# A chunked RWKV-7 and GELU-MLP kernel: the MLP cut into eight pieces between the small products of the next chunk, and the first two inverses on two engines

**Chip, cores, metric.** One core of one Trainium2 chip. The metric is the device time of one execution in microseconds (us). A time quoted is the median of a kernel's runs. Every profile is of one execution; all that the text rests on are of the fast state unless it says otherwise.

## The reference

Four sequences of 768 steps, eight heads of 40. A recurrence per head, then an MLP with an exact GELU over the 320 features:

```python
for t in range(S):
    y[:, :, t] = np.einsum('bhd,bhde->bhe', rt, state)
    Sa = np.einsum('bhde,bhe->bhd', state, at)
    state = state * wt[:, :, None, :] - np.einsum('bhd,bhe->bhde', Sa, bt)
    state = state + np.einsum('bhd,bhe->bhde', vt, kt)
x = y.transpose(0, 2, 1, 3).reshape(B * S, H * D)
h = x @ w_in                                   # 320 -> 2048
out = (0.5 * h * (1.0 + erf(h / sqrt(2)))) @ w_out   # 2048 -> 320
```

## The kernel before

The steps are taken in 12 chunks of 64. In a chunk the recurrence is matrix products plus the inverse of a triangular matrix made of `N`. The names that the argument needs:

- `N`: 64 small products on TensorE, masked on VectorE, stored to DRAM by 8 DMAs, read back as `Nb`.
- the inverse: 62 dependent small operations on GpSimd give `W`; `W` is stored to DRAM (`inv`), read back as `Tt` and `T2`; VectorE transposes a part of it into `L`; TensorE makes `J` from `L` and `J2` from `J`, which completes `Tt`.
- the small stages that use it: `X`, `RV`, `sap`, `saT`, `A`, `M`, `y2`, `QY`, then `xt`, the input of the MLP, made on VectorE and rearranged by DMAs from SP and ScalarE.
- the MLP: `ph` (4 x 40 products of `xt` with `w_in`), gelu on ScalarE, `po` (two halves of 32 products with `w_out`), copied to `os` and stored.
- for the chunk after: loads of w, a, k, b, v, r (32 DMA issues, all on SP), `sums` (the products `cum`, copied to `cs`), transposes `wT`, `aT`, `nT`, `kT`, `vT`, `rT`, `tn`.

The order of TensorE and of SP (the engine that issues DMAs) is that of the program text. VectorE, ScalarE and GpSimd get their order from the scheduler at build time.

```python
def invert(c):
    Nb = work.tile([P, BL, BL], FP32, tag="Nb", name="Nb")        # one buffer per tag
    W = work.tile([P, BL // 2, BL], FP32, tag="W", name="W")
    ...                                                            # Nb <- DRAM on SP
    for j in range(BL - 1):
        tmp = work.tile([P, BL * BL // 7], FP32, tag="tmp", name="tmp")
        ...
        nc.gpsimd.tensor_tensor(t, W[...], Nb[...], ALU.mult)
        nc.gpsimd.tensor_tensor(W[:, :rows, j + 1:], W[:, :rows, j + 1:], t, ALU.add)

def down(c, g):                                                    # up(c): the four ph groups
    po = duo("po")[:, 0, :DM]
    for f in range(NF):
        nc.tensor.matmul(po, gts[c][:, f, g * P:(g + 1) * P], w_out_sb[:, f], ...)
    os = work.tile([P, DM], FP32, tag="os", name="os")
    nc.vector.tensor_copy(os, po)
    ...                                                            # two stores on SP
```

The loop (`n` is the next chunk, `n + 1` the one after; the conditions at the ends are cut):

```python
for c in range(NCH):
    make_N(n); invert(n)
    load_wa(n + 1)
    make_X(c); make_RV(n); make_sa(c); make_A(n)
    make_M(c); make_y2(c); make_QY(c, 0); make_QY(c, 1)
    outputs(c)                                  # xt and the state
    make_av(n)
    down(c - 1, 1)
    load_kb(n + 1); load_v(n + 1); load_r(n + 1)
    up(c)
    sums(n + 1)
    fetch_inverse(n)                            # store W, load Tt and T2, all on SP
    down(c, 0)
    corner(n)                                   # L and J
    turns_a(n + 1); turns_b(n + 1); turn_state()
    joined(n)                                   # J2
```

## Time and profile before

| before | | read from |
|---|---|---|
| time | 936.18 us (935.42 to 937.65, 3 runs) | the runs |
| TensorE busy | 759.0 us, 81% | page, part 1 |
| one chunk, steady | 69.44 us | VectorE's time order: the masks of `N` of chunks 3 and 11 start at 260.90 and 816.40, over 8 |
| mask of `N` of chunk 2 | 193.11 | the same |
| from the mask of chunk 11 to the end | 118.8 | 935.2 - 816.40 |
| `ph` idle for `xt` | 19.0 us in all | page, part 5 |

The "period" below is always that third line, from each kernel's own trace. It is a measure that does not mix the start and the end with the steady chunks. The chain and the queue of one chunk are in the prediction. One thing more is needed later, the end of the inverse on TensorE, from its time order (start, duration, instruction, and in brackets the idle time before it and what ended it):

```profile
457.95 0.74 PE L98 MATMUL J<-L,N 32*32 32x32 f32 x64 [2.53 <-DVE L L428]
458.62 1.75 PE L282 MATMUL wT_ps<-ident,cs_pad 128*128 128x128 f32 x8
460.64 1.88 PE L282 MATMUL aT_ps<-ident,a_pad 128*128 128x128 f32 x8 [0.27 <-ACT part L274]
```

TensorE stands for 2.5 us until L is there, and the two groups of transposes after it take 1.75 and 1.88 us, where the five groups after them take 1.04.

### The profile page before, as it was taken

The page shows a single profiled execution, that of the slowest core. Times are in us where ns is not written, and L with a number is a line of the kernel's source. Part 1 is how long each engine was busy: PE and PEld are TensorE (multiplying, and loading weights), DVE is VectorE, ACT ScalarE, POOL GpSimd, SP SyncE. Part 2 cuts the span into 40 slices and gives each one's busy share as a digit, 9 for nine tenths or more (in the row PEclk, how much of TensorE's full clock was granted, in tenths as well). Part 3 has the DMA queues.
Part 4 walks back from the last instruction along what each step waited for, and adds up shares of the span by engine and source line. Part 5 has one row for each costly group of instructions (what it writes and reads, how often), then busy time and mean ns, then how long its engine had stood idle before and what let it go on. Part 6 is the DMA issues. An engine that isn't in the chain of part 4 may idle for free.

```text
span 935.2 us, 29736 instructions
## 1 busy us (share of the span) xinstructions
PE 759.0 (81%) x13256; PEld 640.0 (68%) x13256; DVE 301.5 (32%) x414; ACT 199.2 (21%) x225; POOL 341.8 (37%) x842
## 2 busy tenths in 40 slices
PE   4343638279879989889889879889899899889898
PEld 3232636278668778688678778778788688778785
DVE  2666788150150240240240250250340330330200
ACT  3020011022222221221221221221322221211110
POOL 4382180118228127127137128127136136136000
PEclk9555769599999979979979889889979979889999
DMA  8677434324233233233233233234233233121100
GB/s 139 116 123 104 93 101 115 58 58 71 48 66 66 46 66 67 45 66 67 45 67 69 43 66 69 42 66 72 41 75 68 38 77 67 32 50 21 24 22 14
DMA packets 255246, 60.40 MB, mean 65 GB/s; under 512 B 241232, under 2 KB 250960, under 8 KB 255120
## 3 DMA queue, kind: packets, MB, share of 16 engines
q1 hardware_dynamic: 251040, 56.22, 32.8%
q10 hardware_dynamic: 4080, 2.30, 1.2%
q8 instruction: 104, 1.70, 0.8%
q14 instruction: 22, 0.18, 0.1%
HBM read 44.30 MB, written 10.22 MB: 58 GB/s over the span
## 4 chain that ended last, share of the span: by engine, by line
PE 52%; SPq 14%; DMA 11%; issue 8%; POOL 6%; DVE 6%; ACT 2%; DVEq 0%; POOLq 0%; ACTq 0%
PE ph L573 15%; PE po L578 13%; SPq L144 5%; PE QY L98 4%; POOL W L397 3%; POOL tmp L395 3%; DMA inv<-W 3%; SPq L414 3%; DMA Tt<-inv 2%; DMA gt<-in_moe_w_in_dram 2%; SPq L133 2%; PE aT_ps L282 2%; SPq L357 2%; PE y_ps L98 2%; PE M_ps L98 2%
## 5 line engine op out<-in xcount | busy, mean ns | idle before, releaser
L395 POOL TENSOR_TENSOR tmp<-W,Nb 128x126 f32<-128x126 f32 (+22 forms) x372 | 143.1, 385 | 282.8 <-DMA Nb<-N 254.6
L573 PE MATMUL ph<-xt,w_in_sb 64*128 64x256 f32 x1920 | 212.1, 379 | 19.0 <-DMA xt<-xt 19.0
L573 PEld LDWEIGHTS ph<-xt,w_in_sb 64*128 64x128 f32 x1920 | 187.0, 188 | 44.3 <-DVE low L231 19.1
L578 PE MATMUL po<-w_out_sb,gt 128*128 128x320 f32 x768 | 212.8, 435 | 2.1 <-DVE w_out_sb L233 2.1
L578 PEld LDWEIGHTS po<-w_out_sb,gt 128*128 128x128 f32 x768 | 144.9, 190 | 62.7 <-DVE w_out_sb L233 2.6
L397 POOL TENSOR_TENSOR W<-W,tmp 128x126 f32<-128x126 f32 (+22 forms) x372 | 147.8, 397 | 29.2
L428 DVE STREAM_TRANSPOSE L<-Tt 128x512 f32<-128x512 f32 x12 | 8.5, 712 | 295.6 <-DMA Tt<-inv 295.6
L570 ACT ACTIVATE gt<-ph 128x1024 f32<-128x1024 f32 x48 | 49.2, 1024 | 222.4 <-PE ph L573 222.4
L302 POOL TENSOR_TENSOR ks<-k_raw,part 128x640 f32<-128x640 f32 x12 | 24.3, 2024 | 86.6 <-ACT part L274 86.6
L98 PE MATMUL J<-L,N 32*32 32x32 f32 x768 | 10.3, 208 | 48.2 <-DVE L L428 48.2
L98 PEld LDWEIGHTS J<-L,N 32*32 32x32 f32 x768 | 9.2, 120 | 54.3 <-issue 53.1
L580 DVE COPY os<-po 128x320 f32<-128x320 f32 x24 | 11.7, 487 | 103.2 <-PE po L578 103.2
L274 ACT ACT_TABLE_LOAD x12 | 15.4, 1283 | 121.6 <-DVE cs_pad L272 121.6
L98 PE MATMUL QY<-VR,ks 64*64 64x104 f32 x768 | 35.4, 340 | 5.4 <-issue 5.4
L98 PEld LDWEIGHTS QY<-VR,ks 64*64 64x64 f32 x768 | 31.8, 198 | 6.8 <-issue 6.8
L387 POOL MEMSET W<- 128x512 f32 x12 | 6.7, 561 | 72.7 <-DMA inv<-W 72.7
L526 DVE TENSOR_TENSOR y<-QY,y 128x512 f32<-128x512 f32 x22 | 15.1, 686 | 54.1 <-PE QY L98 42.0
L98 PE MATMUL cum<-w_raw,cum_m 128*128 128x320 f32 x48 | 18.4, 512 | 12.2 <-DMA k_raw<-in_k_dram 9.3
L318 POOL COPY VR<-v_pad 128x320 f32<-128x320 f32 x24 | 11.1, 472 | 44.4 <-DMA v_pad<-in_v_dram 44.4
L98 PE MATMUL M_ps<-rT,saT 40*64 40x64 f32 x768 | 22.3, 261 | 5.9 <-issue 4.3
L487 ACT COPY saT<-saT_ps 128x512 f32<-128x512 f32 x12 | 7.0, 586 | 92.9 <-issue 80.9
L98 PE MATMUL saT_ps<-Tt,part 64*64 64x64 f32 x704 | 20.2, 271 | 6.9 <-issue 6.9
(105 smaller groups left out, 1004.2 us busy)
## 6 DMA issues: line engine op xcount, KB each, us to landing
Nb<-N SPq DMA_DIRECT2D x24, 256.0 KB
wo_raw<-in_moe_w_out_dram SPq DMA_DIRECT2D x16, 320.0 KB
w_raw<-in_w_dram SPq DMA_DIRECT2D x48, 80.0 KB
k_raw<-in_k_dram SPq DMA_DIRECT2D x48, 80.0 KB
b_raw<-in_b_dram SPq DMA_DIRECT2D x48, 80.0 KB
v_pad<-in_v_dram SPq DMA_DIRECT2D x96, 40.0 KB
r_pad<-in_r_dram SPq DMA_DIRECT2D x96, 40.0 KB
out_dram<-os SPq DMA_DIRECT2D x48, 80.0 KB
```

The costliest lines, as they stand in the source:

```text
L98: nc.tensor.matmul(o, lhsT, rhs, start=first, stop=True, skip_group_check=True)
L133: eng.dma_start(out=t[half(e), g], in_=rows_of(src, c, g, e))
L144: eng.dma_start(out=t[half(e), g, y::2, :D], in_=rows[:, NP * y:NP * (y + 1)])
L282: nc.tensor.transpose(pt[:, g, n], src(g, n), ident)
L302: nc.gpsimd.tensor_tensor(ks[:, :, :, :D], raws.pop((c, "k")), rwv, ALU.mult)
L357: nc.sync.dma_start(out=blk[x, e, z].rearrange("n s t -> s n t"), in_=N[at:at + BL, x, :, :, z * BL:(z + 1) * BL].rearrange("p g n t -> p ...
L395: nc.gpsimd.tensor_tensor(t, W[:, :rows, j:j + 1].to_broadcast([P, rows, rest]), Nb[:, j:j + 1, j + 1:].to_broadcast([P, rows, rest]), ALU ...
L397: nc.gpsimd.tensor_tensor(W[:, :rows, j + 1:], W[:, :rows, j + 1:], t, ALU.add)
L414: nc.sync.dma_start(out=flat_T[at + z * BL:at + (z + 1) * BL, x, :, z * BL:(z + 1) * BL], in_=inv[x, e, z].rearrange("n s t -> s n t"))
L570: nc.scalar.activation(gt[:, 4 * q:4 * q + 4].rearrange("p (s x) t -> p x s t", x=2), ph, ACT.Gelu)
L573: nc.tensor.matmul(o, lhsT, rhs, start=kt == 0, stop=kt == NK - 1)
L578: nc.tensor.matmul(po, gts[c][:, f, g * P:(g + 1) * P], w_out_sb[:, f], start=f == 0, stop=f == NF - 1)
```

## The change

The intent: put dense MLP work between the small products, so that TensorE neither waits for their evacuation nor loses its clock. The MLP of a chunk becomes a generator of 8 pieces, and `fill()` puts one into the order of TensorE. The pieces go "a chunk behind": the last four stand between the small stages of the next chunk. All loads move ahead of `xt`. At the start, the inverse of chunk 0 goes to VectorE so that it can run beside that of chunk 1 on GpSimd.

```diff
-    def invert(c):
+    def invert(c, eng):             # GpSimd's operations become eng's
...
+    def mlp(c):
+        for q in range(NF // 4):
+            ...                     # 40 ph products, gelu
+            yield
+        for g in range(G):
+            ...                     # 16 po products, yield, 16 more, os, stores
+            yield
...
-        if more:
+        if more and c:
             make_N(n)
-            invert(n)
-        if more2:
-            load_wa(n + 1, nc.sync)
+            invert(n, nc.gpsimd)
         make_X(c)
+        fill()
+        if more2:
+            load_w(n + 1); load_a(n + 1); load_kb(n + 1); load_v(n + 1); load_r(n + 1)
         if more:
             make_RV(n)
         make_sa(c)
+        fill()
+        make_saT(c)
         if more:
             make_A(n)
+        fill()
         make_M(c)
         make_y2(c)
+        fill()
         make_QY(c, 0)
         make_QY(c, 1)
         outputs(c)
+        if c == 0:
+            first_convert(4); second_weights(0, 8)
+        pieces.append(mlp(c))
+        fill()
         if more:
             make_av(n)
-        if c:
-            down(c - 1, 1)
-        ...                         # loads of k, b, v, r
-        up(c)
         if more2:
             sums(n + 1)
+        fill()
         if more:
             fetch_inverse(n)
-        down(c, 0)
+        if more2:
+            turns_a(n + 1)
+        fill()
         if more:
             corner(n)
         if more2:
-            turns_a(n + 1)
             turns_b(n + 1)
         if more:
             turn_state()
+        if c == 0:
+            second_weights(8, NF)
+        fill()
+        if more:
             joined(n)
```

The start is reordered as well: `invert(0, nc.vector)`, the loads and `N` of chunk 1 right behind it, `invert(1, nc.gpsimd)`, and the conversion of the weights mostly after `joined(0)`. `N` of chunk 1 gets another buffer; `Nb`, `W` and `tmp` do not. Cut here.

More of the change, by code (lines that the diff above doesn't have):

```diff
@@ L147, in fetch_padded, with load_w, load_a @@
         raws[c, n] = t
-    def load_wa(c, other):
+    def load_w(c):
         fetch(c, "w", w, nc.sync)
-        fetch_padded(c, "a", a, other, False)
+    def load_a(c, eng=nc.sync):
+        fetch_padded(c, "a", a, eng, False)
     def load_kb(c):
@@ L155, in load_kb, with load_v @@
         fetch(c, "b", b, nc.sync)
-    def load_v(c):
-        fetch_padded(c, "v", v, nc.sync, True)
+    def load_v(c, eng=nc.sync):
+        fetch_padded(c, "v", v, eng, True)
     def load_r(c):
@@ L163 @@
     ctx.enter_context(tc.manual_schedule(engines={mybir.EngineType.PE, mybir.EngineType.SP}))
-    load_wa(0, nc.scalar)
+    load_w(0)
+    load_a(0, nc.scalar)
     load_kb(0)
@@ L185 @@
     ks_ring, nb_ring = (ring(n, 2, [P, G, H, HP], pads, nc.gpsimd) for n in ("ks", "nb"))
-    N_ring = ring("N", 1, [P, 2, G, NP, C], None, None)
     VR_ring = ring("VR", 2, [P, 2, G, NP, VC], None, None)
@@ L349, in make_N @@
         t = turned_in[c]
-        N = t["N"] = N_ring()
+        N = t["N"] = work.tile([P, 2, G, NP, C], FP32, tag="turned" if c == 1 else "N", name="N")
         masked(flat(N), products("N_ps", t["nT"], t["aT"], True))
@@ L386, in invert @@
         W = work.tile([P, BL // 2, BL], FP32, tag="W", name="W")
-        nc.gpsimd.memset(W, 0.0)
+        eng.memset(W, 0.0)
         for par in range(2):
             nc.sync.dma_start(out=Nb[par * n:(par + 1) * n], in_=blk)
-            nc.gpsimd.memset(W[par * n:(par + 1) * n].rearrange("p s t -> p (s t)")[:, par::BL + 2][:, :BL // 2], 1.0)
+            eng.memset(W[par * n:(par + 1) * n].rearrange("p s t -> p (s t)")[:, par::BL + 2][:, :BL // 2], 1.0)
         for j in range(BL - 1):
@@ L394, in invert @@
             t = tmp[:, :rows * rest].rearrange("p (s t) -> p s t", s=rows)
-            nc.gpsimd.tensor_tensor(t, W[:, :rows, j:j + 1].to_broadcast([P, rows, rest]),
+            eng.tensor_tensor(t, W[:, :rows, j:j + 1].to_broadcast([P, rows, rest]),
                                     Nb[:, j:j + 1, j + 1:].to_broadcast([P, rows, rest]), ALU.mult)
-            nc.gpsimd.tensor_tensor(W[:, :rows, j + 1:], W[:, :rows, j + 1:], t, ALU.add)
+            eng.tensor_tensor(W[:, :rows, j + 1:], W[:, :rows, j + 1:], t, ALU.add)
         inverses[c] = W
@@ L480, in make_sa, with make_saT @@
                               sap.rearrange("p x y g a d -> p x (y g a) d"))
+    def make_saT(c):
+        t = turned_in[c]
+        xs, Tt = t["xs"], t["Tt"]
         pt = duo("saT_ps").rearrange("p r (k x t) -> p r k x t", k=G * NA, x=2)
@@ L558 @@
     gts = {}
-    def up(c):
+    def mlp(c):
         xt = xts.pop(c)
-        gt = gts[c] = gt_tile()
+        gt = gt_tile()
         for q in range(NF // 4):
@@ L568, in up, with fill @@
                     for x in range(2):
-                        mm_up(ph[:, x, s], w_in_sb[half(x), kt, p * P:(p + 1) * P], xt[half(x), kt], kt)
+                        nc.tensor.matmul(ph[:, x, s], w_in_sb[half(x), kt, p * P:(p + 1) * P], xt[half(x), kt],
+                                         start=kt == 0, stop=kt == NK - 1)
             nc.scalar.activation(gt[:, 4 * q:4 * q + 4].rearrange("p (s x) t -> p x s t", x=2), ph, ACT.Gelu)
-    def mm_up(o, lhsT, rhs, kt):
-        nc.tensor.matmul(o, lhsT, rhs, start=kt == 0, stop=kt == NK - 1)
-    def down(c, g):
-        po = duo("po")[:, 0, :DM]
-        for f in range(NF):
-            nc.tensor.matmul(po, gts[c][:, f, g * P:(g + 1) * P], w_out_sb[:, f], start=f == 0, stop=f == NF - 1)
-        os = work.tile([P, DM], FP32, tag="os", name="os")
-        nc.vector.tensor_copy(os, po)
-        for e in range(2):
-            row = (G * g + e) * S + c * C
-            nc.sync.dma_start(out=out[row:row + C], in_=os[half(e)])
-    first_load(0)
-    first_load(1)
-    load_v(0)
-    sums(0)
-    turns_a(0)
-    make_N(0)
-    invert(0)
+            yield
+        for g in range(G):
+            po = duo("po")[:, 0, :DM]
+            for f in range(NF):
+                nc.tensor.matmul(po, gt[:, f, g * P:(g + 1) * P], w_out_sb[:, f], start=f == 0, stop=f == NF - 1)
+                if f == NF // 2 - 1:
+                    yield
+            os = work.tile([P, DM], FP32, tag="os", name="os")
+            nc.vector.tensor_copy(os, po)
+            for e in range(2):
+                row = (G * g + e) * S + c * C
+                nc.sync.dma_start(out=out[row:row + C], in_=os[half(e)])
+            yield
+    pieces = []
+    def fill(n=1):
+        while n and pieces:
+            if next(pieces[0], "end") == "end":
+                pieces.pop(0)
+            else:
+                n -= 1
+    first_load(0)
+    load_v(0, nc.scalar)
+    sums(0)
+    load_w(1)
+    turns_a(0)
+    load_kb(1)
+    make_N(0)
+    load_a(1)
+    invert(0, nc.vector)
+    first_load(1)
     load_r(0)
+    sums(1)
+    turns_a(1)
+    make_N(1)
+    invert(1, nc.gpsimd)
     turns_b(0)
@@ L596 @@
     make_av(0)
-    first_convert(0)
-    first_load(2)
-    first_convert(1)
-    load_wa(1, nc.sync)
-    load_kb(1)
-    first_load(3)
-    sums(1)
-    turns_a(1)
+    fetch_inverse(0)
     load_v(1)
-    first_convert(2)
-    first_load(4)
     load_r(1)
     turns_b(1)
-    first_convert(3)
-    first_convert(4)
-    fetch_inverse(0)
-    corner(0)
-    joined(0)
-    second_weights(0, 4)
+    corner(0)
+    first_convert(0)
+    first_convert(1)
+    joined(0)
+    first_load(2)
+    first_convert(2)
+    first_load(3)
+    first_convert(3)
+    first_load(4)
     for c in range(NCH):
@@ L618 @@
         more, more2 = n < NCH, n + 1 < NCH
-        if more:
+        if more and c:
             make_N(n)
-            invert(n)
+            invert(n, nc.gpsimd)
+        make_X(c)
+        fill()
         if more2:
-            load_wa(n + 1, nc.sync)
-        make_X(c)
+            load_w(n + 1)
+            load_a(n + 1)
+            load_kb(n + 1)
+            load_v(n + 1)
+            load_r(n + 1)
         if more:
@@ L627 @@
         make_sa(c)
+        fill()
+        make_saT(c)
         if more:
             make_A(n)
+        fill()
         make_M(c)
         make_y2(c)
+        fill()
         make_QY(c, 0)
         make_QY(c, 1)
+        outputs(c)
         if c == 0:
-            second_weights(4, 8)
-        outputs(c)
+            first_convert(4)
+            second_weights(0, 8)
+        pieces.append(mlp(c))
+        fill()
         if more:
             make_av(n)
-        if c == 0:
-            second_weights(8, NF)
-        if c:
-            down(c - 1, 1)
-        if more2:
-            load_kb(n + 1)
-            load_v(n + 1)
-            load_r(n + 1)
-        up(c)
         if more2:
             sums(n + 1)
+        fill()
         if more:
             fetch_inverse(n)
-        down(c, 0)
+        if more2:
+            turns_a(n + 1)
+        fill()
         if more:
@@ L659 @@
             turn_state()
+        if c == 0:
+            second_weights(8, NF)
+        fill()
+        if more:
             joined(n)
-    down(NCH - 1, 1)
+    fill(1000)
 _INS = ['r', 'k', 'v', 'w', 'a', 'b', 'moe_w_in', 'moe_w_out']
```

## The prediction

> **What bounds the kernel now.** I read the page, then the chain of waits, then the time order of TensorE and of the DMA-issuing queue (SP) through one steady chunk.
>
> ```profile
> PE 759.0 (81%) x13256; PEld 640.0 (68%) x13256; DVE 301.5 (32%) x414; ACT 199.2 (21%) x225; POOL 341.8 (37%) x842
> PEclk9555769599999979979979889889979979889999
> ```
>
> The reader is to see that TensorE is busy but not full, and that no other engine is near its limit. The clock row dips once per chunk: TensorE is slowed there as well as idle.
>
> The chain of waits, in order of time, around one steady chunk:
>
> ```profile
> 398.21 1.09 PE N_ps L98 x64
> ...
> 446.81 8.63 PE po L578 x32
> 455.43 0.10 SPq L414
> 455.53 0.04 issue
> 455.57 1.69 DMA Tt<-inv
> ...
> 466.89 0.68 PE J L98 x50
> 467.57 1.09 PE N_ps L98 x64
> ```
>
> N comes at 398.21 and again at 467.57: one chunk takes 69.4 us. Over the nine chunks from N at 191.53 to N at 814.81 the mean is 69.25. Dense MLP work is some 35.2 of it (ph 17.5, po twice 8.8). The rest is small products, at 0.9 to 1.1 us a stage where the clock is full (N above) and about 1.7 where it is half. If all were dense and fast, a chunk would cost about 56: 35.2, eleven stages of 1.0 to 1.4, seven groups of transposes of 0.87, J twice. That 13 us is what the change is after. But just before J the chain goes over to a DMA, so I followed that. The queue in time order:
>
> ```profile
> 401.05 4.80 SPq L357 DMA_DIRECT2D N<-N  x8
> 408.28 1.12 SPq L389 DMA_DIRECT2D Nb<-N  x2
> 409.51 3.12 SPq L133 DMA_DIRECT2D w_raw<-in_w_dram  x4
> 412.68 3.18 SPq L146 DMA_DIRECT2D a_pad<-in_a_dram  x4
> 421.05 0.85 SPq L533 DMA_DIRECT2D xt<-xt  x1
> 421.94 2.81 SPq L536 DMA_DIRECT2D xt<-xt  x4
> ...
> 435.95 5.25 SPq L144 DMA_DIRECT2D v_pad<-in_v_dram  x8
> 441.30 6.07 SPq L144 DMA_DIRECT2D r_pad<-in_r_dram  x8
> 447.47 1.27 SPq L406 DMA_DIRECT2D inv<-W  x2
> 450.83 0.81 SPq L414 DMA_DIRECT2D Tt<-inv  x2
> ```
>
> The inverse is a serial path beside the MLP: N, mask, 8 stores, a load, the elimination on GpSimd (in its time order 413.9 to 442.0, so 28.1), store, load, L on VectorE at 457.09, J at 457.95. N to J takes 59.7 us, of which 5.5 (442.0 to 447.5) is SP still issuing loads. J to the next N takes 9.6. So the 69.3 is the inverse path plus the small stages after it, not TensorE's work. Any new order must shorten that loop.
>
> **What the Trainium skill says.** (1) "DMA: Bandwidth & Descriptors", Issuing engines are not separate DMA queues: issuing from another engine saves only the sequencer's time to initiate it, "usually small relative to the DMA itself". Here that time is not small: four loads of w_raw held SP for 3.12 us, eight of r_pad for 6.07. (2) "SBUF — State Buffer", The DMA setup-cost knee: about 2 us fixed per transfer. The trace agrees: the store of W was issued by 448.74 and what waits for it began at 450.83, 2.1 later. (3) "TensorE: Matmul & The Clock Gate", Part 1: after an idle window of about 3.4 us the array drops to half clock. The trace agrees in kind: the clock is 0.50 in the stretches with long DMA waits, yet also in small stages with gaps of 1 to 1.5 us. (4) Same page, Architectural detail: ScalarE and VectorE are strictly first-in first-out. The order of VectorE below rests on it.
>
> **The change, part by part.** I take durations from the trace and the order from the built program.
>
> *Pieces.* A chunk's 160 ph products become 4 pieces of 4.4 us, its two po halves 4 of 4.4. The po pieces of chunk c-1 stand after X, sap, A and y2. The evacuation waits there are covered and the clock should hold: N, X, po, RV and sap, po, saT and A, po, M and y, po, QY twice: about 28 us from N to the end of QY.
>
> *The new wait.* "A chunk behind" is not true of the first ph piece: in the built order ph of chunk c follows QY of chunk c at once, and needs xt, which needs y, two multiplies and DMAs. Before, av and 8.8 us of po stood there. Also all five loads moved ahead of xt on SP. From N: mask done and stores begun at 3.2, stores to 8.0, Nb to 11.6, loads 21 to 23.6 (sum of the rows of w, a, k, b, v, r in this chunk; 21 with no crowding), 4 output stores of 0.58: xt is issued at 35 to 37.5, though its data is there by about 32. With 0.86 + 2.7 of issue and 1.7 to land, the last part arrives at 40 to 42.5. TensorE stands still from 28 for about 10 us, and starts ph half clocked. First ph piece done about 45, av and cum 47, second piece 52, wT and aT 53.5.
>
> *The inverse path.* From N: 15.7 to GpSimd's first product (413.9-398.2) + 0.4 (ScalarE has a gelu ahead of the Tt copy that the mask waits for) + 28.1 + 3.5 (store, no longer behind loads) + 5.7 issue + 0.6 landing = 54.0 for L. This saves about 5. But VectorE has L ahead of nb, which nT needs: L 0.7, nb 0.8: 55.5. Then on TensorE nT 1.0, ph piece 4.4, J 0.7, kT vT rT tn 3.5, ph piece 4.4, J2 0.65 = 14.7 in place of 9.6. Period 55.5 + 14.7 = **70.2**, against 69.25. The saving is given back by two dense pieces that now stand on the loop. The TensorE/xt path reaches the same place at 53.5, so it nearly binds too.
>
> *Start.* Nb, W and tmp have one buffer each, so the second inverse can't start until the first is done and stored: "at once" doesn't happen. On VectorE the first is 62 products of 92 elements on average, by 0.157 fixed + elements/0.96 per us (fitted to rows: 320 elements 0.49, 1024 1.23) 0.25 each, 16 us instead of 36 (36.95 to 73), but with conversions of 7.3, masks and transposes in its order I get done at about 71. Then v and r of chunk 1 are loaded only after it, and J waits for them: J at 95 against 90.26. xt of chunk 0 stands on SP behind 40 loads, 8 of them waiting for a conversion: about 142 against 127.67. The 16 w_out conversions (23.84/8 = 3.0 each) all come after it, from 148, and N of chunk 2 stands on SP behind the last of them: 148 + 14 x 3.0 + 8.7 of chunk work + 6 to 8 of waits = 206, against 194.37.
>
> *End.* Before, N(11)'s stores at 819.5 to 935.2: 115.7. After: to J2 61.4, less 3.2; then X to QY with four po pieces 26, xt 8.5 uncovered (no loads ahead), ph 17.5 + 1.7 cold, po 17.5, out 2.5: about **131**.
>
> *Sum.* 206 + 9 x 70.2 + 131 = **969**.
>
> **Rivals.** *A: TensorE is the bound and filling it pays.* Removing waits, a chunk could fall to 60: 206 + 540 + 120 = 866, or 900 with half of it. For it: TensorE has 81% of the span, the clock dips. Against: N to J is a chain of DMA and GpSimd that pieces don't touch, and TensorE's order puts two pieces after it. *B: xt's wait is longer than I think.* If crowding or a half clock after the 10 us stop adds 3 us, the TensorE path passes the inverse path: 73 a chunk, 995. For it: loads and xt go out together. Against: loads were already issued at that spacing. *C: the inverse path comes out shorter* (nb not held, shorter stores, 68 a chunk), and the start loses nothing: 194 + 612 + 131 = 937, the same. For it: GpSimd was slowed by VectorE at the start of the elimination and may be less so.
>
> **Range and chances.** The period carries 9 times over: 1.5 us either way is 13.5; the start is good to 8, the end to 5, together about 17. I shade the middle from 969 to **964**, since C errs on the likelier side, and take 938 to 988. The 2% bounds are 917.5 and 954.9. Faster 0.06, same 0.26, slower 0.68.
>
> **What would show it.** Right: N to N about 70; xt issues on SP straight after the loads, ph's idle time (19.0 before) rising to 80 or more with xt's DMA as its cause; the clock down at that point and high in the small stages; L still waiting on Tt; the second elimination starting only after the first; J of chunk 0 after 92; N(2)'s stores after 200. Wrong: if N to N is under 66, the inverse path was not the loop I take it for; if ph does not wait for xt, the order argument fails; if N(2)'s stores are before 190, the start was misjudged.

## The result, and the profile after

After: **996.62 us** (993.56 to 1002.49, 4 runs); before, in the same rounds, 936.91. The ratio is **1.064** (95% interval 1.058 to 1.070): slower. A ratio is the mean of one kernel's fast runs over that of the other's of the same rounds, so not quite the ratio of the medians quoted.

The page after, busy time and clock rows:

```profile
PE 747.5 (75%) x13256; PEld 609.4 (61%) x13256; DVE 317.6 (32%) x479; ACT 236.5 (24%) x254; POOL 301.7 (30%) x777
PEclk9655658788898898997997997997997997998989
```

TensorE does the same 13256 products in 11.5 us less, although the `ph` products take 34 us more (246.5 for 212.1 in part 5 of the two pages) and the `po` products 12 more (224.7 for 212.8). So the small stages gained from the pieces as intended: from N to QY in the chunk below the granted clock is 1.00, where it was 0.77 from 398 to 428 in the kernel before. Yet the clock still dips once per chunk, and the span is 60 us longer. TensorE's time order in the chunk from 428 to 500, after:

```profile
428.31 1.16 PE L98 MATMUL N_ps<-aT,nT 40*64 40x64 f32 x64
...
456.06 1.61 PE L98 MATMUL QY<-SM,nb 64*64 64x104 f32 x64
470.32 6.16 PE L576 MATMUL ph<-xt,w_in_sb 64*128 64x256 f32 x40 [12.65 <-DMA xt<-xt]
...
484.21 1.04 PE L284 MATMUL aT_ps<-ident,a_pad 128*128 128x128 f32 x8
485.08 1.04 PE L284 MATMUL nT_ps<-ident,nb 128*128 128x128 f32 x8
```

Everything from N to QY runs without a stop. Then TensorE stands for 12.65 us, and the first piece of `ph` takes 6.16 us, where the other pieces take 4.59: it starts at half clock (granted clock 0.50 from 470.3 to 473.5). `nT` comes right behind `aT`, with no wait for `nb`; that is so in every one of the eight steady chunks. The queue SP in the same stretch, after:

```profile
457.10 5.62 SPq L144 DMA_DIRECT2D r_pad<-in_r_dram  x8
462.82 4.45 SPq L590 DMA_DIRECT2D out_dram<-os  x4
467.38 0.84 SPq L540 DMA_DIRECT2D xt<-xt  x1
...
471.12 1.28 SPq L409 DMA_DIRECT2D inv<-W  x2
```

This is the place that in the kernel before had `xt` behind a's loads and 15 us ahead of v's (421.05 and 435.95). Now `xt` stands behind all 32 loads and four output stores. VectorE's time order, same stretch, after:

```profile
465.64 0.49 DVE L587 COPY os<-po 128x320 f32<-128x320 f32 x1 [6.27 <-DMA out_dram<-os]
466.05 0.68 DVE L535 TENSOR_TENSOR xt<-y,wpT 128x512 f32<-128x512 f32 x1
...
481.66 0.71 DVE L431 STREAM_TRANSPOSE L<-Tt 128x512 f32<-128x512 f32 x1 [1.97 <-DMA Tt<-inv]
482.30 1.84 DVE L303 SCALAR_TENSOR_TENSOR nb<-b_raw,part 128x640 f32<-128x640 f32 x1
```

VectorE makes L from 481.66, and `nb`, which `nT` needs, stands behind it and is ready at 484.14. The second `xt` product is held too: in VectorE's order it stands behind an output copy, which waits until the previous store has read the only `os` buffer.

**Where the 60 us are.** The masks of `N` split the span into four stretches, and the differences add up to the difference of the spans (995.3 - 935.2 = 60.1):

| stretch | before | after | difference |
|---|---|---|---|
| start to the mask of chunk 2 | 193.11 | 207.89 | +14.8 |
| chunk 2 to chunk 3 | 67.79 | 75.50 | +7.7 |
| chunks 3 to 11, eight periods | 8 x 69.44 | 8 x 72.41 | +23.8 |
| chunk 11 to the end | 118.8 | 132.6 | +13.8 |

So the steady chunks, which the pieces were meant to shorten, are 3.0 us longer each, and the rest loses 36 us more: the start, and an end in which a whole MLP now stands behind the last small stages.

### The profile page after: what moved, and what is told of

Read it like the earlier page. It is cut to its first block, busy times and chain, and to the rows that moved or that the text cites. A ratio compares the mean times of both kernels' runs of the same rounds, so it can differ in the third digit from the quotient of the medians.

```text
span 995.3 us, 29674 instructions
## 1 busy us (share of the span) xinstructions
PE 747.5 (75%) x13256; PEld 609.4 (61%) x13256; DVE 317.6 (32%) x479; ACT 236.5 (24%) x254; POOL 301.7 (30%) x777
## 4 chain that ended last, share of the span: by engine, by line
PE 64%; SPq 12%; DMA 10%; DVE 10%; issue 4%; POOL 0%; ACTq 0%; DVEq 0%; ACT 0%; POOLq 0%
PE ph L576 22%; PE po L583 19%; SPq L144 6%; DMA xt<-xt 3%; PE QY L98 2%; DMA out_dram<-os 2%; PE J L98 2%; SPq L133 2%; SPq L590 1%; PE saT_ps L98 1%; PE RV_ps L98 1%; PE cum L98 1%; PE A_ps L98 1%; PE M_ps L98 1%; PE kT_ps L284 1%
## 5 line engine op out<-in xcount | busy, mean ns | idle before, releaser
L576 PE MATMUL ph<-xt,w_in_sb 64*128 64x256 f32 x1920 | 246.5, 414 | 150.5 <-DMA xt<-xt 150.5
L576 PEld LDWEIGHTS ph<-xt,w_in_sb 64*128 64x128 f32 x1920 | 207.3, 207 | 182.4 <-issue 160.5
L583 PE MATMUL po<-w_out_sb,gt 128*128 128x320 f32 x768 | 224.7, 446 | 5.9 <-DVE w_out_sb L235 5.5
L398 POOL TENSOR_TENSOR tmp<-W,Nb 128x126 f32<-128x126 f32 (+22 forms) x341 | 125.1, 367 | 342.6 <-DMA Nb<-N 316.6
L400 POOL TENSOR_TENSOR W<-W,tmp 128x126 f32<-128x126 f32 (+22 forms) x341 | 130.2, 382 | 26.7
L322 DVE COPY vT<-vT_ps 128x1024 f32<-128x1024 f32 x12 | 14.7, 1224 | 54.9 <-PE vT_ps L284 54.9
L328 DVE TENSOR_TENSOR SM<-M_ps,upper 128x1024 f32<-128x1024 f32 x12 | 14.7, 1224 | 50.2 <-PE M_ps L98 50.2
L328 DVE TENSOR_TENSOR VR<-RV_ps,upper 128x1024 f32<-128x1024 f32 x12 | 14.7, 1223 | 44.6 <-PE RV_ps L98 44.6
L284 PE MATMUL vT_ps<-ident,v_pad 128*128 128x128 f32 x96 | 14.5, 298 | 16.7 <-DMA v_pad<-in_v_dram 16.7
L308 DVE TENSOR_TENSOR aT<-aT_ps,wpT 128x1024 f32<-128x1024 f32 x12 | 14.7, 1224 | 33.7 <-ACT wpT L306 27.5
```

The costliest lines, as they stand in the source:

```text
L284: nc.tensor.transpose(pt[:, g, n], src(g, n), ident)
L328: nc.vector.tensor_tensor(to, pt, upper.unsqueeze(1).to_broadcast([P, 2 * G * NP, C]), ALU.mult)
L398: eng.tensor_tensor(t, W[:, :rows, j:j + 1].to_broadcast([P, rows, rest]), Nb[:, j:j + 1, j + 1:].to_broadcast([P, rows, rest]), ALU.mult)
L400: eng.tensor_tensor(W[:, :rows, j + 1:], W[:, :rows, j + 1:], t, ALU.add)
L576: nc.tensor.matmul(ph[:, x, s], w_in_sb[half(x), kt, p * P:(p + 1) * P], xt[half(x), kt], start=kt == 0, stop=kt == NK - 1)
L583: nc.tensor.matmul(po, gt[:, f, g * P:(g + 1) * P], w_out_sb[:, f], start=f == 0, stop=f == NF - 1)
```

## The experiments

All outputs are right. The kernel before was run beside each, between 926.8 and 950.3 us.

### The start, undone: oldstart

```diff
-    first_load(0); load_v(0, nc.scalar); sums(0); load_w(1); ...; invert(0, nc.vector); ...
+    first_load(0); first_load(1); load_v(0); sums(0); turns_a(0); make_N(0); invert(0, nc.gpsimd); ...   # as before
```

> The changed kernel's loop behind the start of the kernel before (first inverse on GpSimd, second in the first round of the loop, weights loaded and converted earlier). It parts the change in two. Theory: of the 60 us lost, about 20 are the start (stores of N of chunk 2 at 214.6 against 194.4), 27 the nine periods and 15 the end. With the old start: 970 to 985. If the start costs nothing: 993 to 998; if it is all of it: 940.

972.32 us, ratio 1.036. The mask of chunk 3 starts at 260.18, where after has 283.39 and before 260.90. The period stays at 72.11. So the new start costs 23 to 24 us, and the loop and the end the rest.

### Truly at once: atonce

The first inverse takes its `Nb`, `W` and `tmp` from tags that are free at that time, so nothing is shared:

```diff
-        Nb = work.tile([P, BL, BL], FP32, tag="Nb", name="Nb")
+        Nb = work.tile([P, BL, BL], FP32, tag="Nb" if c else "xt", name="Nb")
```

(and the same for `W` with "L" and `tmp` with "Js").

> The changed kernel with separate buffers for Nb, W and tmp of chunk 0, so that the first two inverses really run at once on VectorE and GpSimd. Theory: the second inverse is not what chunk 1 waits for (the conversions of w_out and the order of the DMA queue are), so starting it 30 us sooner gains nothing: within 4 us of the changed kernel. The elimination on VectorE gets slower, by contention, by up to 5 us, and that may cost as much. Rival (the missing overlap is what the start lost): 20 us faster, about 975.

997.84 us, ratio 1.063: no gain. The overlap does happen: GpSimd's first product of chunk 1 starts at 58.97, in the changed kernel at 75.78, while VectorE is at chunk 0 until 69.4, 0.6 later than in the changed kernel (68.8), so the slowing that was feared there was small. But `xt` of chunk 0 is issued at 149.61, in the changed kernel at 147.86. The inverse was not what the start waited for. After it, this is the queue SP in the changed kernel:

```profile
151.28 24.74 SPq L260 DMA_DIRECT2D wo_raw<-in_moe_w_out_dram  x8
...
186.43 28.12 SPq L260 DMA_DIRECT2D wo_raw<-in_moe_w_out_dram  x8
214.60 3.89 SPq L360 DMA_DIRECT2D N<-N  x8
```

The 16 loads of `w_out` alternate with their conversion on VectorE through two buffers, and the stores of `N` of chunk 2 stand behind the last. That these loads are what the start lost is read from the queue; no run moves them alone. In oldstart, four of them went at 89.82, before the loop, and these stores came at 189.87.

### The output buffer: os2

```diff
-            os = work.tile([P, DM], FP32, tag="os", name="os")
+            os = (work.tile([P, LW], FP32, tag="top", name="os")[:, :DM] if c and g
+                  else work.tile([P, DM], FP32, tag="os", name="os"))
```

> The changed kernel with a second buffer for the output tile os of the second half of each chunk (it uses a tile that is free after the weights are converted). In the changed trace the second os copy waits for the first output store to land, and the second xt product stands behind that copy on VectorE. If that is on the path: the four output stores take 2.4 us of the queue in place of 4.45, xt is issued about 2 us sooner, the wait of ph falls from 12.6 to about 10.5 a chunk, and the period from 72.5 to about 70.5, where the loop through the inverse stops it: 975 to 982. If only the loads ahead of it on the queue matter, no change: 993 to 998.

985.76 us, ratio 1.049, period 70.80, `ph` idle 133.8 us against 150.5. The wait for the single buffer is worth 1.6 us a chunk; the gain in time is a little under what was expected.

### Two pieces later: lag2

Chunk 0 skips its last two fills, so every later chunk has its pieces two places later; the first `ph` piece then stands behind `nT`, and `xt` has time to land:

```diff
             turns_a(n + 1)
-        fill()
+        fill(1 if c else 0)          # here, and at the next fill()
```

> The changed kernel, but chunk 0 leaves out its last two pieces, so that every later piece stands two places further on: the last two po pieces of chunk c-1 now stand between QY and the first ph piece of chunk c. Theory L (the loop through the inverse, N to N, sets the period; the wait for xt only adds to it): the wait of ph for xt, 150 us in all, falls under 30; J then waits for L instead, N to L stays about 54 us, and with one ph piece, not two, between L and the next N the period falls from 72.5 to about 64, in all 915 to 930. Theory T (TensorE is the bound, all it loses is the wait for xt): the wait goes and nothing takes its place, period about 60, under 890. If the wait for xt is not what costs, the time stays at 990 or more.

958.01 us, ratio 1.023, period 67.82: less gained than expected. `ph` waits once only, 35.5 us in the first chunk. In its place TensorE's time order has this, in the chunk from 412:

```profile
469.15 1.08 PE L98 MATMUL J<-L,N 32*32 32x32 f32 x64 [5.96 <-DVE L L431]
470.16 1.97 PE L284 MATMUL kT_ps<-ident,ks 128*128 128x128 f32 x8
```

As soon as `xt` no longer binds, the inverse does: J waits for L, and the transposes after it run at half clock. GpSimd was done at 454.0, but SP came to the store of `W` only at 457.86: ahead of it in SP's order was an output store, whose `po` piece ended at 456.07.

### N a piece earlier: nahead and nahead_lag2

```diff
-        if more and c:
-            make_N(n)
-            invert(n, nc.gpsimd)
         make_X(c)
...
             turns_a(n + 1)
+            make_N(n + 1)
+            invert(n + 1, nc.gpsimd)
```

(with a second buffer for `N`). N then does not wait for J, J2 and two pieces that it does not need.

> The changed kernel with the loop through the inverse cut: N of chunk c+2 and its elimination are started right after the transposes that N needs, before J of chunk c+1, with a second buffer for N. The pieces stay where they are, so ph still waits for xt. Theory L: the changed period is held by two paths that nearly tie, the inverse and the wait for xt; with the inverse off the path the xt wait alone remains. The loads now start about 8 us earlier on the queue, so xt leaves when its data is ready: period about 68, wait of ph 90 to 110 in all, 950 to 965. Theory T (only TensorE's order and its waits matter, the inverse is hidden): no change of more than 10 us from 996.

971.82 us over its four runs, 970.71 over the three fast ones, ratio 1.029, which is above the range expected. Its profiled run fell in the slow state (1000.4 us), so nothing is read from its trace; where the missing microseconds went in this version stays open.

With lag2 as well:

> Both: the loop through the inverse cut, and the pieces two places further on (as lag2). Theory L: nothing but TensorE's own work is left, 56 us a chunk if dense and at full clock: period 58 to 61, 865 to 890, L no longer waited for. If a third bound stands behind these two (the DMA queue issues some 43 us a chunk, GpSimd is busy 31), the period stays at 63 or more: over 905.

926.77 us, ratio **0.983** (0.978 to 0.989), period 64.14: 1.1 to 2.2% faster than before, but above the 865 to 890. The expectation named this outcome as a third bound.

### The same with the old start: nahead_old

> As nahead_lag2, behind the start of the kernel before. If the new start costs 24 us whatever the loop does (996 against 972 in oldstart), this is 20 to 25 faster than nahead_lag2: 845 to 868. If the start's loss is made up by the faster loop, as the same as nahead_lag2.

912.76 us, ratio 0.967, period 64.52. The old start gives back 14 us, not the 20 to 25 expected; the period is hardly changed. TensorE's time order shows where the third bound bites:

```profile
571.87 1.08 PE L98 MATMUL J<-L,N 32*32 32x32 f32 x64 [3.89 <-DVE L L431]
```

J waits for L, and SP, where the store of `W` of the chunk after is issued:

```profile
616.19 2.92 SPq L543 DMA_DIRECT2D xt<-xt  x4
624.26 1.15 SPq L590 DMA_DIRECT2D out_dram<-os  x2
625.51 1.26 SPq L409 DMA_DIRECT2D inv<-W  x2
```

GpSimd's last operation on `W` of that chunk ended at 608.8. SP was free from 619.1, but had an output store next, whose data came at 624.2, and the store of `W` stood behind it. The inverse waited 16.7 us, of which 6.4 behind that store.

### The store of the inverse ahead: inv_early, inv_split and lag2_inv

inv_early is nahead_old with the store and the loads of the inverse issued earlier:

```diff
         if more:
             make_av(n)
+            fetch_inverse(n)
         if more2:
             sums(n + 1)
         fill()
-        if more:
-            fetch_inverse(n)
```

> The best version so far (nahead_old, 65 a chunk) with the store and loads of the inverse issued right after av, ahead of the piece whose output store they stood behind: there GpSimd was done at 608.8 and SP came to the store of W at 625.5, as it waited in its own order for the last po piece and its copy. Theory (SP's order is what still binds, J waits 3.9 us for L and TensorE then runs three transposes at half clock): J's wait under 2 us, 60 to 62.5 a chunk, 865 to 888 us. Rival (the clock or GpSimd binds): 63.5 or more, over 895.

873.22 us, ratio **0.928**, period 60.91. As expected.

inv_split has the store of `W` ahead of `xt`, and the loads of the inverse behind it.

> The same with the store of W ahead of xt on SP and only the loads of the inverse behind xt. If SP's order still costs something with the store behind xt, this is 5 to 15 us faster than inv_early. In the built order VectorE has L ahead of the mask of N here, so if that holds N back the gain is lost: equal or slower than inv_early.

**858.10 us, ratio 0.914** (0.909 to 0.919), period 59.45: the fastest. TensorE's time order there:

```profile
600.05 1.16 PE L98 MATMUL N_ps<-aT,nT 40*64 40x64 f32 x64 [1.10 <-ACT nT L310]
...
605.66 0.76 PE L98 MATMUL J<-L,N 32*32 32x32 f32 x64
606.35 1.09 PE L284 MATMUL kT_ps<-ident,ks 128*128 128x128 f32 x8
```

J does not wait, the transposes run at full clock, and in the whole chunk from 541.58 to 600.05 the only idle time listed on TensorE is the 1.1 us before N. The clock is at 0.9 or more in every slice of the steady chunks. VectorE's L ahead of the mask of N cost nothing that shows.

The same move on lag2 alone, without N ahead and with the new start:

> lag2 (the last two pieces of a chunk one place later, 67.8 a chunk, where 64 had been expected) with the store and loads of the inverse ahead of the piece whose output store held them up: GpSimd was done at 454.0 and the store of W issued at 457.9. Theory (the miss of lag2 was SP's order): the store comes some 4 us sooner, J waits 2 us at most, 63.5 to 65 a chunk, 920 to 935 us. Rival (half clock or VectorE's order held it): over 945.

925.25 us, ratio 0.988, period 64.27. Time and period are as expected: J's wait is down from 5.96 to 2.31 us in the chunk looked at, and from 5.9 to 2.9 on average over the eight steady chunks. So lag2's miss was for the most part SP's order; the wait that is left is above the 2 us expected.

### Loads out of the way of xt: loads_early and akb_early

These ask whether the inverse path in the changed order is really as long as the prediction summed it. The loads of the chunk after next are issued at the end of a chunk, where SP has nothing to do. TensorE's order is untouched.

```diff
-            load_w(n + 1); load_a(n + 1); load_kb(n + 1)
             load_v(n + 1); load_r(n + 1)
...
             joined(n)
+        if n + 2 < NCH:
+            load_w(n + 2); load_a(n + 2); load_kb(n + 2)
```

Chunk 0 also keeps these loads at their old place, for chunk 2.

> The changed kernel with one thing moved: the loads of w, a, k and b of the chunk after next are issued at the end of a chunk, where SP has nothing else to do, so that only v and r still stand ahead of xt. The order of TensorE is not touched. Theory (xt's late issue sets the period of 72.5 by a hair over the inverse path): the idle time of ph falls from 150 to under 70 us in all, and then the inverse path binds at what the prediction gave it, L at 54 after N, nb behind L, then nT, one piece, J and so on: 70 a chunk, 970 to 982 us. Rival (xt's wait is the whole of the loss, and the inverse has slack in this order): 62 to 66 a chunk, 900 to 940. Rival (loads are not what holds xt): no change, 990 or more.

1052.86 us, ratio 1.121, period 77.1. None of the three was right. `ph`'s wait did fall, to 109.2 us, but the time order of ScalarE shows a new one:

```profile
437.81 1.28 ACT L269 ACT_TABLE_LOAD   x1 [10.31 <-DMA w_raw<-in_w_dram]
...
441.15 1.02 ACT L578 ACTIVATE gt<-ph 128x1024 f32<-128x1024 f32 x1
```

The scheduler's order, with w loaded earlier, has its logarithm (L269, with its table load) ahead of a gelu and an exponential that the running chunk needs. ScalarE takes its work in order, so they wait 10 us for a load they have no use for.

akb_early leaves w where it was:

> The first attempt at moving loads failed for another reason: ScalarE's built order put the logarithm of the newly loaded w ahead of the gelu and the exponential that the chunk needed. Here w stays where it was and only a, k and b are issued at the end of a chunk; the built order of ScalarE hardly changes, and VectorE has the output copy ahead of the xt products. The xt DMAs should then be issued when their data is there, 5 to 6 us sooner. Theory (two paths of nearly one length, xt's the longer by a little): xt's wait falls to 6 to 7 us a chunk, the inverse path takes over with L about 54 after N and 70 to 71 a chunk, 970 to 985 us. Rival (xt's wait is the whole loss, the inverse has slack): 67 or less, under 955.

987.16 us, ratio 1.056, period 69.58. TensorE's time order:

```profile
469.34 7.44 PE L576 MATMUL ph<-xt,w_in_sb 64*128 64x256 f32 x40 [6.38 <-DMA xt<-xt]
...
487.06 1.09 PE L284 MATMUL nT_ps<-ident,nb 128*128 128x128 f32 x8 [1.51 <-DVE nb L303]
```

The wait for `xt` is halved, 12.65 to 6.38 us, and the period falls by 2.8 only. On VectorE, L starts at 485.58, 51.9 after N (433.67), nb stands behind it, and the chain of waits runs from N through the DMAs, GpSimd, L and nb to `nT`. `nT` waits for `nb` in six of the eight steady chunks (1.0 to 3.4 us), where in the changed kernel it never does. So the inverse path is now the longer one in most chunks, and the period on it is about 69.6. The time is a little above the range expected because the first chunks lost 12 us (mask of chunk 3 at 295.67, after 283.39); why was not looked into.

### The kernel before, with its own loop loosened: before_nahead and rlate

before_nahead moves `N` ahead in the kernel before, as nahead does in the changed one:

```diff
+        if more2:
+            turns_a(n + 1)
+            make_N(n + 1)
+            invert(n + 1)
         down(c, 0)
...                                  # their old places are taken out; the first N of the loop stays
         if more:
             corner(n)
```

> The kernel before, its MLP whole, with only the loop cut: N of chunk c+2 and its elimination start before J of chunk c+1, second buffer for N. Theory L: J's wait of 2.5 us for L and part of what it costs in clock go, but the small stages still run one after another with their waits: period 64 to 67 against 69.3, 900 to 920. If the loop was the whole bound of the kernel before: period near 58, 840. If it was none: 937, no change.

1018.62 us, ratio 1.082, period 78.50: far off. VectorE's time order:

```profile
483.46 0.71 DVE L428 STREAM_TRANSPOSE L<-Tt 128x512 f32<-128x512 f32 x1 [27.36 <-DMA Tt<-inv]
484.10 0.79 DVE L272 COPY cs_pad<-cum 128x640 f32<-128x640 f32 x1
```

The products `cum` were ready at 474.3, but their copy stands behind L in VectorE's order. So wT, aT, nT and the new N, all of which the edit meant to run before the inverse, wait for the inverse of the chunk before; TensorE stands for 10.71 us. The data no longer tied N to L; the queue of an engine did.

rlate moves only the eight loads of r behind the store and loads of the inverse:

```diff
-            load_r(n + 1)
         up(c)
...
             fetch_inverse(n)
+        if more2:
+            load_r(n + 1)
```

> The kernel before with the eight loads of r moved behind the store and loads of the inverse on SP. GpSimd was done at 442.0 in the chunk looked at and SP came to the store at 447.5. Theory (before is bound by N to J through the inverse, 5.5 of it SP issuing loads): the store comes 5 us earlier, J then waits for the po half instead, some 2.3 us sooner: 66.5 to 67.5 a chunk, 910 to 922 us. Rival (TensorE's own work binds before): within 5 us of 937.

895.60 us, ratio **0.953** (0.947 to 0.959), period 65.16: more than expected. TensorE's time order:

```profile
441.47 0.75 PE L98 MATMUL J<-L,N 32*32 32x32 f32 x64
442.15 1.09 PE L282 MATMUL wT_ps<-ident,cs_pad 128*128 128x128 f32 x8
443.08 1.04 PE L282 MATMUL aT_ps<-ident,a_pad 128*128 128x128 f32 x8
```

Against the same lines of before: the wait of 2.53 us is gone, 0.27 before aT is gone, and wT and aT are 0.66 and 0.84 shorter at full clock. That makes 4.3, and the difference of the periods is 4.28 (69.44 - 65.16). Over all eight steady chunks the split is much the same: the transposes take 50.7 us in place of 66.4 (2.0 a chunk), and TensorE stands idle for 33.7 in place of 52.5 (2.3 a chunk). The expectation had counted the wait and not the clock.

## Why the prediction was right or wrong

**Right: the direction and the loop.** "Any new order must shorten that loop", with N, the inverse, and the stages after it as the loop, is what the runs bear out. The pieces alone gained nothing in time, and five versions of it that shorten the loop have ratios below 1: nahead_old, inv_early and inv_split are faster by more than 2%, lag2_inv is the same within 2%, and nahead_lag2 lies on the 2% line. rlate shows the same for the kernel before. Rival A (the waits filled, 866 to 900) is refuted for this change, though its 60 us a chunk is what inv_split reaches (59.45) once nothing else binds.

**Right in size: the inverse path.** "55.5 + 14.7 = 70.2" was given as the period. With `xt`'s wait halved, akb_early runs at 69.58, mostly on that path. The parts were less exact. The prediction had L begin at 54.0 after N, and `nb` done at 55.5; in the changed kernel L began at 53.3 (481.66 - 428.38) and `nb` was done at 55.8, as it took 1.84 us and not 0.8. In the chunk of akb_early shown, L began at 51.9.

**Wrong: which of two nearly equal paths is longer.** "The TensorE/xt path reaches the same place at 53.5, so it nearly binds too." The place is `nT`, which waits for both. Measured from N at 428.38:

| step | predicted | measured |
|---|---|---|
| loads end on SP | 33 to 35 | 34.3 |
| `xt` issued | 35 to 37.5 | 39.0 |
| `ph` starts | 40 to 42.5 | 41.9 |
| first `ph` piece done | 45 | 48.1 |
| `wT` and `aT` done | 53.5 | 56.7 |
| nb ready (inverse path) | 55.5 | 55.8 |

The failed step is this 53.5: the path over TensorE and `xt` reached `nT` 3.2 us later than predicted. 1.8 of it is the first piece, put at 4.4 us, although the prediction itself says that TensorE "starts ph half clocked"; it took 6.16. 1.3 is the start of `ph`: a first piece done at 45 means a start at 40.6, the early end of the prediction's own 40 to 42.5. Behind that start two errors nearly cancel. The four output stores were put at 4 x 0.58 = 2.3 us; they held SP for 4.45, as the second pair had to wait for the single `os` buffer (os2 gives 1.6 us a chunk back). But `ph` began 2.9 us after the first issue of `xt`, where the sum had 5.3 until the last part had landed: it starts while SP is still issuing the last part (470.4). In all, the `xt` path is 0.9 longer than the inverse path, not 2 shorter. The nine periods from the stores of chunk 2 (214.60) to those of chunk 11 (863.91) come to 72.15 each in place of 70.2: +17.5 us. This is rival B, with its 73 a chunk. Of its two causes the half clock is there; crowding does not show, as the loads ended within the range predicted, and the wait of the output stores was not named. That its total of 995 us came true is luck: it kept the start at 206, which was 8.6 short, and put the nine periods 7.7 too long.

**Wrong: the start.** The stores of `N` of chunk 2 were put at 206 and came at 214.60: +8.6. The loads of `w_out` began at 151.3 for 148 (`xt` of chunk 0 had been issued at 147.86 for 142). The two groups took 24.7 + 28.1 = 52.9 us in place of 14 x 3.0 = 42, and the rest of that stretch 10.4 in place of 16: +3.3, +10.9 and -5.6. That the two inverses would not overlap was right in mechanism, and J of chunk 0 was at 94.36 for 95; but atonce shows that the overlap would not have mattered, so that reasoning carried no time.

**Right: the end.** 131 predicted, 131.4 measured (863.91 to 995.3), with errors that cancel: its terms add to 132, `xt` left TensorE idle for 5.5 in place of 8.5, and the output after the last product took 4.1 in place of 2.5. The 115.7 given there for the kernel before is misread: the stores of `N` of chunk 11 begin at 817.65, not 819.5, which makes 117.6; the 969 does not rest on it.

**The sum.** 206 + 9 x 70.2 + 131 = 969 was short by 8.6 + 17.5 + 0.4 = 26.5, which gives the 995.3 of the trace. The range of 938 to 988 was the second error: it was shaded downward on the ground that rival C "errs on the likelier side", while the text had one path 2 us behind another. With two paths this close, an error of more than 2 us on the shorter one lengthens the loop, while a shorter inverse path can save 2 us at most, so the range should have leaned up.

**Not settled.** Why nahead alone gained no more, and the 12 us that akb_early lost in its first chunks. And what the pieces themselves are worth: no working run has N ahead and the early store without the pieces (before_nahead failed by VectorE's order), so the 0.914 of inv_split is that of the whole series.

## What to carry to other kernels

When a loop has several paths of nearly one length, removing the wait that the profile shows uncovers the next one: here `xt`, then the inverse behind an output store on SP, then TensorE itself, and of the versions with pieces only inv_early and inv_split beat the 0.953 that rlate reaches without them. Read an in-order queue as a path of its own: for each transfer on the loop, ask what stands ahead of it and whether that one's data is there, and after every edit look at what the scheduler did to the order of VectorE and ScalarE. Before a large reordering, try the small one: moving eight loads behind one store took the kernel before to 0.953 of its time.

## What the Trainium skill lacked or had wrong

- "DMA: Bandwidth & Descriptors", Issuing engines are not separate DMA queues: the time to initiate a DMA is "usually small relative to the DMA itself". Here the issues add up: the 32 load issues of a chunk, 0.74 us each on average, held SP for some 24 us (439.10 to 462.72 in the changed kernel), and the eight of r, moved alone, were worth 4.3 us a chunk. The page does not work out what an issue whose data is not there yet costs those behind it: in nahead_old one output store held a finished `W` back for 6.4 us, and putting the store and loads of the inverse ahead was worth 3.6 us a chunk (64.52 to 60.91).
- "TensorE: Matmul & The Clock Gate", Part 1: half clock comes after an idle window of about 3.4 us. Here the length of one stop did not decide it. In the kernel before, the granted clock fell to 0.50 after a stop of 2.53 us (from 459.0 on) and also after one of 1.76 (at 664.7 to 666.4; the transposes from 667.1 on took 1.97 and 1.75 us); in akb_early a stop of 3.37 us (415.2 to 418.5) left the clock at 1.00 and the next transposes at 1.09. In both cases of the kernel before, 0.7 us of small J products stood between the stop and the fall.
- No page that I read speaks of what the order that a scheduler gives VectorE and ScalarE can cost. Loading one tensor earlier put its logarithm ahead of a needed gelu, which ScalarE then held for 10.3 us (loads_early); L ahead of a ready copy made TensorE stand for 10.7 us (before_nahead).
